# Loading K and V two heads at a time, with half as many keys per head in a loop step, in a decode attention kernel

## The chip, the cores and the metric

One core of a Trainium2 chip (the rounds of runs fell on several chips; a ratio compares kernels of the same round). The metric is the time of one execution on the device, in microseconds, taken over several executions. A profiled span is about 1.8 us shorter than the time (80.7 and 82.5 us for the kernel before). Runs marked slow (over 1.5% above the fastest of the same kernel) are left out of ratios.

## The reference

One token (D = 512) goes through layer norm; the result xn feeds an attention over the last 4096 keys of a cache and a small gated MLP. The output is the sum of both and the residuals.

```python
W = 4096                                  # window of the cache, Sk = 65536
q = (xn @ wq)                             # 32 heads of 128; wq is 4.2 MB in bf16
k = k_cache[:, :, Sk - W:, :]             # 8 heads of 4096 x 128: 8.4 MB
v = v_cache[:, :, Sk - W:, :]             # 8.4 MB; 4 query heads share one head of K and V
p = softmax(q @ k.T * 128 ** -0.5)
attn = (p @ v) @ wo                       # wo 4.2 MB
mlp  = (silu(xn @ w_gate) * (xn @ w_up)) @ w_down   # F = 1792, 1.8 MB each; scaled by sigmoid(xn . w_r)
out  = x + attn + xn + mlp
```

## The kernel before

30.7 MB come in through one queue in the order wq, K, V, gate, up, wo, w_down. Each head of K is one transfer of 1 MB: partition p holds 32 keys (8 KB) of that head.

```python
t_k = [dma(sy, f"k{g}", k_sb[:, g].rearrange("p b (i d) -> p (b i) d", d=DH),
           A_k_cache[0, g, Sk - W:, :].rearrange("(p t) d -> p t d", t=NT)) for g in range(HKV)]
```

The score loop takes one head per step. A head is four blocks of 1024 columns. Each block is copied into a buffer at a fixed address (C, VectorE), transposed on TensorE (T, eight transposes), copied out of PSUM (E, VectorE or ScalarE), and multiplied by q (Sm, two matmuls of 512 columns). In Sm the 32 weight columns are placed at one of four strips of the array, `tile_position=(0, 32 * cq)`:

```python
def Sm(b, i, q, last=False):
    te.wait_ge(s_ev[b], i)
    for e in range(2):
        c = 2 * b + e
        cq, ch = c % 4, c // 4                 # blocks 2 and 3: strips 0,1,2,3; so blocks 0 and 1
        ins = te.matmul(sc[32 * cq:32 * cq + 32, ch, :], lhsT=q[:], rhs=kT[:, b, e * 512:(e + 1) * 512],
                        start=False, stop=False, tile_position=(0, 32 * cq), skip_group_check=True)
    ...
with te.Fori(1, 9) as i:                       # one head per step
    T(0, i); T(1, i)
    te.wait_ge(s_qb, i); Sm(2, i, qB); Sm(3, i, qB, last=True)     # blocks of the step before
    T(2, i); T(3, i)
    te.wait_ge(s_qa, i); Sm(0, i, qA); Sm(1, i, qA, last=True)
```

Then softmax, a loop over heads for P times V (called PV; VectorE copies V and the probabilities into fixed buffers, TensorE multiplies, ScalarE brings the result back), gate and up, and 46 matmuls of one weight column (32 for wo, 14 for w_down).

## Time and profile before

| | before |
|---|---|
| time, median (lowest to highest), first 4 runs | 82.47 us (82.34 to 82.54) |
| profiled span | 80.7 us |
| first transpose of K | 16.52 us |
| scores ready | 42.49 us |
| PV done | 61.3 us |
| first wo matmul | 65.46 us |
| last piece of wo landed | 72.84 us |
| last matmul ended | 77.8 us |

In the timeline a line reads: start in us, length in us, engine, line of the kernel, operation, output<-inputs, how many instructions were merged, and in brackets how long the engine was idle before them and what ended that. The length of merged matmuls includes the latency of the last; the step to the next line's start tells the throughput.

### The profile page before, as it was taken

The numbers are of one execution on the slowest core, as the hardware profiler recorded it, in microseconds if no ns is written. First come the engines' busy times: TensorE is split into PE (matmuls) and PEld (weight loads), VectorE is DVE, ScalarE is ACT, GpSimd is POOL, SyncE is SP. The second block draws the span as 40 slices with busy tenths as digits, with TensorE's granted clock in tenths as the row PEclk, the third lists the DMA queues.
The fourth block names the chain that finished last, engine by engine and source line by source line (L and its number), as shares of the span: only waits on it lengthen the run. The fifth ranks groups of instructions, "written<-read, shape, count | busy, mean of one in ns | idle before, by whom it ended". The sixth has DMA issues, their size and how long they took to land.

```text
span 80.7 us, 1552 instructions
## 1 busy us (share of the span) xinstructions
PE 60.5 (75%) x596; PEld 29.9 (37%) x596; DVE 43.5 (54%) x103; ACT 29.7 (37%) x40; POOL 7.3 (9%) x27
## 2 busy tenths in 40 slices
PE   0012945589999999999988968877888887788950
PEld 0012201386657768667732323222233322123300
DVE  3775000195678977968736678888763380000030
ACT  1941001305696896895860422442222200000000
POOL 5910000101112112121200000000000000000000
PEclk9999999555799999999999999999999999999999
DMA  1899998999999999999999999999999999999400
GB/s 33 309 439 390 455 447 374 434 418 434 418 430 410 434 410 430 414 434 406 430 410 430 406 430 414 445 447 412 426 419 413 418 426 418 416 402 398 138 2 1
DMA packets 4185, 30.72 MB, mean 381 GB/s; under 512 B 467, under 2 KB 598, under 8 KB 1110
## 3 DMA queue, kind: packets, MB, share of 16 engines
q1 hardware_dynamic: 4178, 30.67, 91.7%
q8 instruction: 2, 0.03, 0.2%
q14 instruction: 1, 0.01, 0.0%
q10 hardware_dynamic: 4, 0.00, 0.0%
HBM read 30.67 MB, written 0.00 MB: 380 GB/s over the span
## 4 chain that ended last, share of the span: by engine, by line
SPq 48%; DMA 40%; PE 6%; issue 2%; DVE 1%
SPq L151 48%; DMA k_sb<-in_A_wo_dram 40%; PE ps L467 4%; PE ps L462 2%; DVE res L471 1%; SPq L500 0%; SPq L74 0%
## 5 line engine op out<-in xcount | busy, mean ns | idle before, releaser
L276 ACT COPY kT<-ps 128x1024 bf16<-128x1024 bf16 x19 | 18.5, 1019 | 8.8 <-PE ps L302 8.7
L302 PE MATMUL ps<-ident_bf,kin 128*128 128x128 bf16 x256 | 18.7, 231 | 0.8 <-DVE kin L268 0.6
L302 PEld LDWEIGHTS ps<-ident_bf,kin 128*128 128x128 bf16 x256 | 15.8, 104 | 5.1 <-issue 4.2
L268 DVE COPY kin<-k_sb 128x1024 bf16<-128x1024 bf16 x32 | 12.2, 422 | 0.7 <-PE ps L302 0.7
L273 DVE COPY kT<-ps 128x1024 bf16<-128x1024 bf16 x13 | 9.0, 692 | 4.4 <-PE ps L302 4.3
L462 PE MATMUL ps<-k_sb,oT 128*1 128x512 bf16 x32 | 7.5, 378 | 2.0 <-DMA k_sb<-in_A_wo_dram 2.0
L394 ACT CAST pvS<-ps 128x512 bf16<-128x512 f32 x8 | 4.7, 586 | 9.6 <-PE ps L399 9.6
L471 DVE TENSOR_TENSOR res<-ps,resid 1x512 bf16<-1x512 f32 x1 | 0.7, 679 | 11.5 <-PE ps L467 11.5
L375 DVE COPY vin<-v_sb 128x2048 bf16<-128x2048 bf16 x8 | 5.5, 686 | 1.4 <-PE ps L408 1.4
L381 DVE COPY vin<-v_sb 128x2048 bf16<-128x2048 bf16 x8 | 5.5, 683 | 0.0
L408 PE MATMUL ps<-vin,pTcur 128*16 128x512 bf16 x32 | 3.1, 381 | 2.6 <-ACT pvS L394 2.2
L462 PEld LDWEIGHTS ps<-k_sb,oT 128*1 128x1 bf16 x32 | 2.4, 83 | 7.1 <-DMA k_sb<-in_A_wo_dram 3.2
L420 PE MATMUL ps<-zmov,zst 128*128 128x512 bf16 x16 | 4.7, 377 | 0.0
L228 PE MATMUL ps<-wq_sb,xnT 128*1 128x512 bf16 x32 | 2.9, 499 | 2.3 <-DMA wq_sb<-in_A_wq_dram 2.3
L310 PE MATMUL ps<-kT,qB 128*32 128x512 bf16 x36 | 4.2, 413 | 0.4 <-ACT kT L276 0.3
L244 DVE COPY qpad<-ps 128x16 bf16<-128x16 bf16 x2 | 0.3, 174 | 7.6 <-PE ps L240 7.6
L310 PE MATMUL ps<-kT,qA 128*32 128x512 bf16 x32 | 4.4, 417 | 0.0
L259 POOL COPY qA<-qpad 128x32 bf16<-128x32 bf16 x8 | 2.0, 255 | 20.6 <-DVE qpad L244 10.9
L194 PE MATMUL ps<-ident_bf,xn_row 1*128 1x1 bf16 x4 | 0.3, 165 | 4.6 <-DVE xn_row L189 4.6
L147 PE MATMUL ps<-zmov,zst 128*128 128x512 bf16 x14 | 3.7, 382 | 0.0
L234 ACT CAST q<-ps 128x512 bf16<-128x512 f32 x2 | 1.1, 589 | 6.6 <-PE ps L228 6.6
L414 PE MATMUL ps<-vin,pTcur 128*16 128x512 bf16 x32 | 3.1, 382 | 0.2 <-DVE vin L381 0.2
(85 smaller groups left out, 50.2 us busy)
## 6 DMA issues: line engine op xcount, KB each, us to landing
k_sb<-in_A_k_cache_dram SPq DMA_DIRECT2D x8, 1024.0 KB, 20.6
v_sb<-in_A_v_cache_dram SPq DMA_DIRECT2D x8, 1024.0 KB, 28.2
wq_sb<-in_A_wq_dram SPq DMA_DIRECT2D x2, 2048.0 KB, 9.5
k_sb<-in_A_wo_dram SPq DMA_DIRECT2D x4, 1024.0 KB, 32.0
wq_sb<-in_B_w_gate_dram SPq DMA_DIRECT2D x1, 1792.0 KB, 29.3
wq_sb<-in_B_w_up_dram SPq DMA_DIRECT2D x1, 1792.0 KB, 31.4
k_sb<-in_B_w_down_dram SPq DMA_DIRECT2D x2, 512.0 KB, 31.4
k_sb<-in_B_w_down_dram SPq DMA_DIRECT2D x1, 384.0 KB, 25.7
```

Source lines behind the costliest of these rows:

```text
L147: te.matmul(ps[:, 7, :], lhsT=zst[:], rhs=zmov[:], start=True, stop=True)
L151: eng.dma_start(out=out_, in_=in_).then_inc(s, 16)
L268: ve.tensor_copy(out=kin[:, b, :], in_=k_sb[:, g, b, :]).then_inc(s_c[b], 1)
L273: ve.tensor_copy(out=kT[:, b, :], in_=tp[:, b, :]).then_inc(s_ev[b], 1)
L276: ac.copy(out=kT[:, b, :], in_=tp[:, b, :]).then_inc(s_ev[b], 1)
L302: ins = te.transpose(tp[:, b, k * P:(k + 1) * P], kin[:, b, k * P:(k + 1) * P], ident_bf[:])
L310: ins = te.matmul(sc[32 * cq:32 * cq + 32, ch, :], lhsT=q[:], rhs=kT[:, b, e * 512:(e + 1) * 512], start=False, stop=False, tile_position= ...
L375: ve.tensor_copy(out=vin[:, 0], in_=v_sb[:, g, 0:16, :]).then_inc(s_va, 1)
L381: ve.tensor_copy(out=vin[:, 1], in_=v_sb[:, g, 16:32, :]).then_inc(s_vb, 1)
L394: ac.copy(out=pvS[:].rearrange("p t d -> p (t d)"), in_=pv_ps).then_inc(s_pvs, 1)
L420: te.matmul(ps[:, 7, :], lhsT=zst[:], rhs=zmov[:], start=True, stop=True)
L462: te.matmul(a_ps, lhsT=oT2[:, j:j + 1], rhs=wo_sb[:, j * D:(j + 1) * D], start=False, stop=False, skip_group_check=True)
```

## The change

Its intent is longer pieces in the transfers: two heads of K (or V) in one transfer of 2 MB, in which partition 2q + h holds 64 keys of head h, 16 KB in a row. A step of the score loop then has 32 keys of each of 64 partitions of two heads, and the two heads need different queries. So each block's two matmuls now separate the even and odd partitions (e), with their own weights. Softmax works on two banks, one for each e. In the PV loop the probabilities are multiplied by a 0/1 column per parity.

```diff
-    t_k = [dma(sy, f"k{g}", k_sb[:, g]..., A_k_cache[0, g, Sk - W:, :].rearrange("(p t) d -> p t d", t=NT)) for g in range(HKV)]
+    def pair(cache, g):
+        return cache[0, 2 * g:2 * g + 2, Sk - W:, :].rearrange("h (q t) d -> q h (t d)", t=TP)   # TP = 64
+    t_k = [dma(sy, f"k{g}", halves(k_sb, g), pair(A_k_cache, g)) for g in range(HP)]             # HP = 4; V alike
 ...
-            c = 2 * b + e
-            cq, ch = c % 4, c // 4
-            ins = te.matmul(sc[32 * cq:32 * cq + 32, ch, :], lhsT=q[:], rhs=kT[:, b, e * 512:(e + 1) * 512],
-                            start=False, stop=False, tile_position=(0, 32 * cq), skip_group_check=True)
+            ins = te.matmul(sc[32 * b:32 * b + 32, e, :], lhsT=qAB[:, e, :],
+                            rhs=kT[:, b, :].rearrange("d (k h q) -> d h k q", h=2, q=PH)[:, e],
+                            start=False, stop=False, tile_position=(0, 32 * b), skip_group_check=True)
 ...
-    ac.activation(out=p_sb[:, h * 512:(h + 1) * 512], in_=sc[:, h, :], func=ACTF.Exp, ...)
+    ac.activation(out=p_sb[:].rearrange("p (j e) -> p e j", e=2)[:, h], in_=sc[:, h, :], func=ACTF.Exp, ...)
 ...
-        ve.tensor_copy(out=pTcur[:]..., in_=pT_ps...[:, :, :, REP * g:REP * (g + 1)]).then_inc(s_pt, 1)
+        for e in range(2):
+            ins = ve.tensor_scalar(out=pTcur[:, :, :, e, :], in0=src, scalar1=par2[:, e:e + 1], scalar2=None, op0=ALU.mult)
```

Cut are the setup of the 0/1 columns and of a permuted identity, the single q buffer, the maximum and bias of softmax for two banks, a sum over the two parities after the PV loop, and the shapes that follow from these.

## The prediction

> **What bounds the kernel now.** I read the strip of the span in 40 slices first, then the chain that ended last, then the timeline of the tail, and at last the timeline of TensorE in the score loop.
>
> ```profile
> PE   0012945589999999999988968877888887788950
> DVE  3775000195678977968736678888763380000030
> DMA  1899998999999999999999999999999999999400
> ...
> 40.85 31.95 DMA k_sb<-in_A_wo_dram
> 72.80 0.04 issue
> 72.84 1.89 PE ps L462 x8
> 74.73 3.10 PE ps L467 x14
> ```
>
> The DMA row is full from 4 us to 75 us, and the chain is one queue of 30.7 MB whose last piece of wo lands at 72.8; then 22 matmuls run one behind the other, and an add. So the transfers set the end. The span is 80.7 us, the time 82.48, so I add 1.8 us to a span. The rate by stage, from windows cut where the summed bytes of the slices change tensor (columns: window, length, engines, granted clock, DMA share, GB/s):
>
> ```profile
> 4.00:12.10 8.10, 3.68 (x24) 1.21 (x24) 2.75 (x10) 1.21 (x3) 0.35 (x2) 1.00 1.02 435
> 12.10:52.10 40.00, 35.22 (x411) 21.74 (x412) 27.75 (x65) 22.16 (x27) 3.90 (x16) 0.91 1.01 420
> 52.10:60.60 8.50, 6.93 (x74) 2.18 (x71) 6.79 (x15) 3.00 (x6) 0.00 (x0) 1.00 1.01 428
> 60.60:70.60 10.00, 8.06 (x64) 2.78 (x63) 3.19 (x7) 1.06 (x2) 0.00 (x0) 1.00 1.00 419
> ```
>
> These are wq (16 KB pieces) 435, K and V (8 KB) 420, gate and up (14 KB) 428, wo (8 KB) 419: longer pieces run some 3% faster. But compute is close behind. Of TensorE's timeline in the score loop (start, length, instructions merged):
>
> ```profile
> 28.00 0.40 PE L310 MATMUL ps<-kT,qB 128*32 128x512 bf16 x4
> 28.33 1.07 PE L302 MATMUL ps<-ident_bf,kin 128*128 128x128 bf16 x16
> 29.33 0.73 PE L310 MATMUL ps<-kT,qA 128*32 128x512 bf16 x4
> ...
> 65.46 1.89 PE L462 MATMUL ps<-k_sb,oT 128*1 128x512 bf16 x8 [0.26 <-DMA k_sb<-in_A_wo_dram]
> ```
>
> Half a loop step is 16 transposes (1.00 us to the next start) and four score matmuls (0.33 us to the next start): 1.33 us, or up to 1.8 where ScalarE's copy is late. Four matmuls of 512 columns take 0.33 us from start to next start, while eight of wo take 1.89 us (7 spacings of 0.216 plus a last of 0.38). Four in 0.33 us cannot have run one by one: they sat on four different 32-column strips (cq = 0, 1, 2, 3) and ran together.
>
> The slack follows: wo's first three pieces need 24 x 0.216 = 5.2 us of TensorE before 72.84, so its start may slip from 65.43 to 67.6 before anything is lost. **Slack 2.2 us.**
>
> **What the Trainium skill says.** "TensorE: Matmul & The Clock Gate", Part 3 (packing small matmuls): matmuls at different tile positions overlap, starting about 4 ns apart, and matmuls start and end strictly in program order. The trace agrees on the overlap (four in 0.33 us). "TensorEngine Tiling (Array Packing)", Key Properties: tiles operate independently; thus matmuls of one strip have nothing to overlap with, as the 0.216 us spacing of wo shows. The first page's Part 1 says that an idle TensorE is given half its clock and wins it back after some 3.4 us of work; here the clock was 0.50 from about 14.3 to 21.2 us, after the idle time that ended at 13.1. "DMA: Bandwidth & Descriptors", Latency and other measured facts, warns of rows at large powers of two; the two heads lie 16 MB apart. No run here shows that yet, and within a head the pieces stay contiguous.
>
> **The change part by part.**
>
> 1. Pieces of 16 KB for K and V: 16.8 MB at 420 GB/s is 39.9 us, at 432 (my choice between 428 and 435) 38.8. The queue shortens by **1.1 us**, if the rate is a matter of piece length.
>
> 2. A first pair must land whole. The shortest time from issue to landing on the K buffer is 13.7 us, and the first K was issued at 1.86: head 0 landed at 15.6, just before the first copy at 16.04. A second MB takes 2.5 us more: 18.0. The first transpose goes from 16.52 to 18.5: **+2.0 us** for compute. Later pairs land every 4.9 us and a pair takes over 7 us of compute, so no further wait.
>
> 3. The score matmuls. Before, block b's two matmuls went to strips 2b and 2b+1 (modulo 4). Now both go to strip b, one for each half of the partitions, in the order 2, 2, 3, 3 (and 0, 0, 1, 1). In program order the second must wait for the first; the third runs beside the second; the fourth waits for the third: three turns in place of one, two more of 0.216 us. A half step is 1.00 + 0.33 + 0.43 = 1.76 us. That also covers ScalarE: five copies of about 1 us in two steps of 3.5. At half clock it is 1.82 (16.52 to 18.34) + 0.55 + 2 x 0.43 = 3.23 us. I take one and a half half steps at half clock (it lasted 4.7 us from the first transpose before; the gate's phase is not known). Sixteen half steps: 1.5 x 3.23 + 14.5 x 1.76 = 30.4 us, where before they took 41.26 - 16.52 = 24.7. **+5.7 us**, with the tail of the scores unchanged.
>
> 4. Softmax: two bias columns and a strided output of the exponential, nothing I can size; all eight transposes wait for the second exponential, **+0.2**. The memset of the output bank (0.48 us) goes, but it was off the path.
>
> 5. The PV loop: a step takes 1.67 us, closed through VectorE's two value copies (0.69, 0.68), the probability copy (0.22), and TensorE and ScalarE. One copy of 128 columns becomes two multiplies by a 0/1 column; consecutive starts of such short operations lie 0.13 us apart, so **+0.14 x 8 = +1.1 us**. The matmuls have 32 columns of weights in place of 16 and the same stream, so 0.33 us still.
>
> 6. Setup: three more VectorE operations (about 0.28 + 0.28 + 0.15) and two more copies of q lie while wq and the first K pair are still on their way: nothing. A single q buffer is refilled during 1.00 us of transposes (copy 0.2 to 0.3 us): nothing.
>
> Sum: compute is later by 2.0 + 5.7 + 0.2 + 1.1 = 9.0 us at the end of PV, 61.26 + 9.0 = 70.3. From there to the first wo matmul it was 4.17 us, of which 0.5 and 0.26 were waits for up and wo, which have landed by now: 3.4, so 73.7. All of wo and nearly all of w_down are there (72.8 and 77.3 less 1.1). Then 46 matmuls: 45 x 0.216 + 0.38 = 10.1, to 83.8, against 77.8 before. **+6.0 us, of which I keep 5.7**, since small waits of the old loop may be absorbed: 82.48 + 5.7 = **88.2 us**. The 1.1 us saved on the queue is not seen, because the end no longer hangs on it.
>
> **The rivals.**
>
> - *The transfers stay the bound.* If compute slipped by under 2.2 us, the end would come 1.1 us earlier: 81.4 us. For it: the DMA row is full, and later wo pieces are each waited for 0.5 to 0.6 us. Against: the first pair alone costs 2.0, and the doubling on one strip is in the diff.
> - *Two matmuls of one strip cost one turn more, not two* (TensorE finding more overlap): 16 x 0.216 = 3.5 us less, 84.7. Against: the order 2, 2, 3, 3 and starts in order.
> - *No overlap at all (four turns)*: +3.5, about 91.7. Against: gate's 16 matmuls took 0.93 us, which needs overlap whenever the strips differ.
> - *Heads 16 MB apart slow the transfers.* At 10% less rate K and V take 4.4 us longer, and w_down lands at 82; then both ends meet near 88. For it only a warning of the skill.
>
> **Range and chances.** The clock's phase is worth 1.5 us either way, the PV step 1 us, the number of turns 3.5 us at small odds. I take 85.2 to 90.4 for 8 in 10, mostly between 86.5 and 89.5. Slower by over 2% (above 84.1) 0.90; within 2% 0.07, which is the rival with two turns and a lucky clock; faster 0.03, for which nearly every step would have to be wrong.
>
> **What would show each step right or wrong.** In the changed kernel's trace: K and V at about 432 GB/s; the first transpose near 18.5 us; four score matmuls spread over some 0.83 us in place of 0.40 and half steps of 1.76; scores ending near 50 us (42.5 before); PV ending near 70; no DMA wait before wo, the DMA row empty over the last 6 us or more, and 46 matmuls in one row of about 10 us. I am wrong if the score matmuls still merge into 0.40 us, if half steps stay at 1.33, or if a DMA is still what wo waits for last.

## More of the kernel before

The lines that carry the reading are in the prediction. Here only the PV loop of the kernel before, TensorE's timeline, of which the prediction has the numbers but not the lines; first matmuls of two successive steps lie 1.68 us apart:

```profile
49.58 0.39 PE L408 MATMUL ps<-vin,pTcur 128*16 128x512 bf16 x4 [0.31 <-ACT pvS L394]
...
51.26 0.39 PE L408 MATMUL ps<-vin,pTcur 128*16 128x512 bf16 x4 [0.31 <-ACT pvS L394]
```

## The result

The changed kernel takes 85.64 us (85.20 to 86.28, 4 runs) against 82.47: a ratio of 1.039, interval 1.031 to 1.047, slower. A ratio is the mean time of one kernel's fast runs over that of the other's fast runs of the same rounds, so it is not quite the ratio of these medians. Two later measurements of the same kernel gave 1.031 (85.75 us) and 1.031 (85.41 us). The prediction was 88.2 us, 85.2 to 90.4: the direction held and the time lies in the range, but at its low end. Of 5.7 us only some 3 came.

From the page of the changed kernel, the span and the slices, with the row of TensorE's granted clock (the share of its full clock that it was given, in tenths):

```profile
span 83.5 us, 1538 instructions
...
PE   0010956709999999999999893798887889999960
...
PEclk9999999999999999999999999759999999999999
DMA  2899999999999999999999999999999999980000
...
PE 59%; DMA 19%; DVE 9%; ACT 6%; issue 2%; SPq 1%; DVEq 0%
```

The DMA row now ends four slices (over 8 us) before the span does, and the last line, the engines' shares of the chain that ended last, puts 59% on TensorE; before, 88% of it was the queue (48% the issuing of its transfers, 40% a transfer of wo). The same window as for K and V before, now to 51.0 us (same columns):

```profile
12.10:51.00 38.90, 34.01 (x362) 20.13 (x362) 23.46 (x55) 21.64 (x25) 2.40 (x8) 1.00 1.01 429
```

429 GB/s in place of 420: the transfers did what was wanted of them. TensorE's timeline, from the score loop, the PV loop and the tail:

```profile
18.62 1.89 PE L316 MATMUL ps<-perm_bf,kin 128*128 128x128 bf16 x16 [1.92 <-DVE kin L282]
20.44 1.04 PE L322 MATMUL ps<-kT,qAB 128*32 128x512 bf16 x4
...
28.18 1.07 PE L316 MATMUL ps<-perm_bf,kin 128*128 128x128 bf16 x16
29.17 0.61 PE L322 MATMUL ps<-kT,qAB 128*32 128x512 bf16 x4
29.72 1.07 PE L316 MATMUL ps<-perm_bf,kin 128*128 128x128 bf16 x16
...
58.36 0.40 PE L419 MATMUL ps<-vin,pTcur 128*32 128x512 bf16 x4 [0.32 <-ACT pvS L406]
...
60.13 0.40 PE L419 MATMUL ps<-vin,pTcur 128*32 128x512 bf16 x4 [0.32 <-ACT pvS L406]
...
70.55 7.07 PE L476 MATMUL ps<-k_sb,oT 128*1 128x512 bf16 x32
77.46 3.19 PE L481 MATMUL ps<-k_sb,hTr 128*1 128x512 bf16 x14
```

The first transpose comes at 18.62. The four score matmuls take 0.61 us and 0.55 us to the next start (0.40 and 0.33 before); a half step is 1.54 us. A step of the PV loop is 1.77 us here, and 1.80 on average of the five from 56.58 to 65.57 (1.68 before). All 32 matmuls of wo run in one row from 70.55 with no wait for a transfer. The first half step and part of the second ran at half speed (16 transposes in 1.89 and 1.57 us, not 1.07), although the row of the granted clock reads full there. The kept trace has no record of the clock before 22.51 us, and the page shows full where there is none; so I go by the durations.

### The profile page after: what moved, and what is told of

Read it like the earlier page. It is cut to its first block, busy times and chain, and to the rows that moved or that the text cites. A ratio compares the mean times of both kernels' runs of the same rounds, so it can differ in the third digit from the quotient of the medians.

```text
span 83.5 us, 1538 instructions
## 1 busy us (share of the span) xinstructions
PE 64.1 (77%) x596; PEld 30.7 (37%) x596; DVE 46.3 (55%) x116; ACT 30.4 (36%) x40; POOL 6.0 (7%) x19
## 4 chain that ended last, share of the span: by engine, by line
PE 59%; DMA 19%; DVE 9%; ACT 6%; issue 2%; SPq 1%; DVEq 0%
PE ps L316 21%; DMA k_sb<-in_A_k_cache_dram 19%; PE ps L322 11%; PE ps L476 8%; PE ps L481 4%; PE ps L425 3%; ACT pvS L406 3%; PE ps L419 3%; DVE vin L392 2%; PE ps L431 2%; ACT p_sb L368 2%; PE ps L453 2%; PE ps L410 2%; DVE vin L384 2%; DVE pTcur L390 1%
## 5 line engine op out<-in xcount | busy, mean ns | idle before, releaser
L316 PE MATMUL ps<-perm_bf,kin 128*128 128x128 bf16 x256 | 18.4, 229 | 1.9 <-DVE kin L282 1.9
L316 PEld LDWEIGHTS ps<-perm_bf,kin 128*128 128x128 bf16 x256 | 15.6, 103 | 9.0 <-issue 6.8
L322 PE MATMUL ps<-kT,qAB 128*32 128x512 bf16 x68 | 11.5, 398 | 0.2 <-ACT kT L290 0.2
L431 PE MATMUL ps<-zmov,zst 128*128 128x512 bf16 x16 | 5.6, 435 | 0.0
L419 PE MATMUL ps<-vin,pTcur 128*32 128x512 bf16 x32 | 3.4, 415 | 2.2 <-ACT pvS L406 1.3
L275 POOL COPY qAB<-qpad 128x64 bf16<-128x64 bf16 x8 | 2.4, 300 | 37.2 <-PE ps L322 37.2
L243 PE MATMUL ps<-wq_sb,xnT 128*1 128x512 bf16 x32 | 3.8, 621 | 1.7 <-DMA wq_sb<-in_A_wq_dram 1.7
L390 DVE TENSOR_SCALAR pTcur<-ps,par 128x128 bf16<-128x128 bf16 x16 | 3.8, 279 | 1.6 <-PE ps L373 1.6
L425 PE MATMUL ps<-vin,pTcur 128*32 128x512 bf16 x32 | 3.5, 430 | 0.4 <-DVE vin L392 0.3
L151 PE MATMUL ps<-zmov,zst 128*128 128x512 bf16 x14 | 3.7, 382 | 0.0
```

Source lines behind the costliest of these rows:

```text
L316: ins = te.transpose(tp[:, b, k * P:(k + 1) * P], kin[:, b, k * P:(k + 1) * P], perm_bf[:])
L322: ins = te.matmul(sc[32 * b:32 * b + 32, e, :], lhsT=qAB[:, e, :], rhs=kT[:, b, :].rearrange("d (k h q) -> d h k q", h=2, q=PH)[:, e], sta ...
L419: ins = te.matmul(pv_ps[32 * tl:32 * tl + 32, :], lhsT=pTcur[:, tl].rearrange("p q e r -> p (q e r)"), rhs=vin[:, 0].rearrange("p (q t) d ...
L425: ins = te.matmul(pv_ps[32 * tl:32 * tl + 32, :], lhsT=pTcur[:, 4 + tl].rearrange("p q e r -> p (q e r)"), rhs=vin[:, 1].rearrange("p (q t ...
L431: te.matmul(ps[:, 7, :], lhsT=zst[:], rhs=zmov[:], start=True, stop=True)
```

## The experiments

Every kernel gave a correct result. "First wo matmul" is the best single mark of how late compute is, since all that follows it is a fixed row unless a transfer is late.

**The changed kernel again (e1, later e10).** No edit; the measure for the others.

> The changed kernel again, as the measure for the others on this chip. 85.6 us (85.2 to 86.3 so far), ratio to before 1.039. TensorE has four score matmuls in two turns (0.54 us to the next start), not three.

> The changed kernel once more for its scatter: 84.5 to 86.3 us, ratio 1.03 to 1.04. Its end hangs on compute, so where the half clock falls shows in the time; before hangs on the queue and stays within 0.5%.

85.75 us (84.56 to 85.91), ratio 1.031, and 85.41 us (84.51 to 86.23), ratio 1.031. The scatter is 1.6 to 2%, while the kernel before stays within 0.5% in all its runs. First wo matmul at 71.02 in the profile of e1. The profile of e10 fell in a slow run; nothing is drawn from it.

**Eight matmuls in one group (e4).** What do two matmuls of one strip cost? A turn is the time that one matmul of 512 columns holds its strip, 0.216 us. My prediction said two more turns; the half step of 1.54 in place of 1.33 says one. This kernel puts all eight score matmuls of a step behind each other, after all their waits.

```diff
-        T(0, i); T(1, i); Sm(2, i); Sm(3, i, last=True); T(2, i); T(3, i); te.wait_ge(s_q, i); Sm(0, i); Sm(1, i)
+        for b in range(4): T(b, i)
+        te.wait_ge(s_q, i)
+        for b in range(4): te.wait_ge(s_ev[b], i)
+        for b in range(4): Sm(b)                    # strips 0,0,1,1,2,2,3,3
```

> A measuring kernel, slower on purpose: all eight score matmuls of a step in one group, strips 0,0,1,1,2,2,3,3, after all waits. Three theories on order. Each strip goes its own way (a matmul of a free strip passes one that waits): two turns, 0.22 + 0.39 = 0.61 us from first start to last end. Neighbours in the program pair up: four turns, 1.04 us. Strict program order, as my prediction assumed: five turns, 1.26 us.

TensorE's timeline of one step, then (cut into stretches, of the score matmuls alone: window, length, TensorE busy and how many were in flight, weight loads, clock, DMA share, GB/s):

```profile
31.20 0.62 PE L321 MATMUL ps<-kT,qAB 128*32 128x512 bf16 x8 [1.22 <-ACT kT L292]
31.76 1.96 PE L316 MATMUL ps<-perm_bf,kin 128*128 128x128 bf16 x32
```

```profile
31.20:31.30 0.10, 0.10 (x4) 0.10 (x8) 1.00 0.77 328
31.30:31.40 0.10, 0.10 (x4) 0.03 (x5) 1.00 0.38 164
31.40:31.45 0.05, 0.05 (x8) 0.00 (x0) 1.00 0.77 328
```

Eight in 0.62 us: four start at 31.20, four more just after 31.40, while the first four still drain, and the transposes follow at 31.76. That is two turns, as if each strip were served by itself. Strict program order (five turns, 1.26 us) and pairs of neighbours (four, 1.04 us) are excluded. The records do not name which of the eight started first, so that a free strip's matmul passes a waiting one is inferred here from the count. The changed kernel's own trace shows it. In the group at 26.00 us the program has two matmuls for one strip, then two for another, and the second pair waits for ScalarE's copy (same columns; windows between the starts):

```profile
25.98:26.08 0.10, 0.08 (x1) 0.08 (x2) 1.00 0.76 328
26.11:26.21 0.10, 0.10 (x2) 0.10 (x2) 1.00 1.15 492
26.24:26.31 0.07, 0.07 (x3) 0.00 (x0) 1.00 0.00 0
```

Both weight loads of the first pair are there at once, but one matmul runs. At 26.10 (these times are of the trace's single records) the weight load that waits for the copy starts, and with it a matmul; the next comes at 26.22, 0.226 us after the first, and the last at 26.32, 0.226 us after the one of 26.10. So the third in the program started before the second, whose strip was taken.

As a kernel e4 is slow, 90.19 us in its one run, because TensorE waits for all four copies in each step.

**Four strips again (e2).** Only the strip of the odd partitions is changed, so that the four matmuls of a group stand on four strips; the PV loop reads those strips in reverse.

```diff
-            ins = te.matmul(sc[32 * b:32 * b + 32, e, :], lhsT=qAB[:, e, :], ..., tile_position=(0, 32 * b))
+            s = 3 - b if e else b
+            ins = te.matmul(sc[32 * s:32 * s + 32, e, :], lhsT=qAB[:, e, :], ..., tile_position=(0, 32 * s))
 ...
-            ve.tensor_scalar(out=pTcur[:, :, :, e, :], in0=src, ...)
+            ve.tensor_scalar(out=pTcur[:, :, :, e, :], in0=src[:, :, ::-1, :] if e else src, ...)
```

> Only the strip of the second half of the partitions is changed (block b of half 1 goes to strip 3-b), so that the four score matmuls of a group stand on four strips again. If strips shared by two matmuls are the largest cost: a group goes from 0.54 to 0.33 us to the next start, half steps from 1.54 to 1.33 to 1.4, 16 of them save 3.3 us of compute, and the end comes about 3.1 us earlier, 82.2 to 82.8. Rival, the cost is the strided read of the keys (64 columns at a stride of 128), which stays: the group stays near 0.54 and the time at 85.6.

83.85 us (83.19 to 83.89), ratio 1.013: 1.9 us less than e1. TensorE's timeline:

```profile
28.24 1.07 PE L316 MATMUL ps<-perm_bf,kin 128*128 128x128 bf16 x16
29.24 0.40 PE L323 MATMUL ps<-kT,qAB 128*32 128x512 bf16 x4
29.57 1.07 PE L316 MATMUL ps<-perm_bf,kin 128*128 128x128 bf16 x16
30.57 0.40 PE L323 MATMUL ps<-kT,qAB 128*32 128x512 bf16 x4
30.90 1.07 PE L316 MATMUL ps<-perm_bf,kin 128*128 128x128 bf16 x16
31.90 0.74 PE L323 MATMUL ps<-kT,qAB 128*32 128x512 bf16 x4
```

The group is back at 0.40 and 0.33, so the strided read of the keys costs nothing that shows. The saving is 1.9 and not 3.1, in part because every fourth group waits for ScalarE again (0.74 us, next transposes 0.79 after its start), as in the kernel before. From the first transpose to the last step's own score matmuls the loop takes 24.8 us here and 26.9 in e1. Sharing strips thus costs 2.1 us of loop. The turns alone come to 3.6 us (13 of 0.21 and two of 0.43 at half clock); late copies give back some 1.0 of it, and 0.5 is the clock, which in e2's profile was half for one half step more (transposes 1.55 us at 23.41; 1.07 at 24.26 in e1).

**The first pair of K in two transfers (e3).** Each has 32 keys of every partition, what one step needs; the other pairs stay.

```diff
-    t_k = [dma(sy, f"k{g}", halves(k_sb, g), pair(A_k_cache, g)) for g in range(HP)]
+    t_k0 = [dma(sy, f"k0{u}", *unit(A_k_cache, k_sb, 0, u)) for u in range(2)]      # 1 MB each, 8 KB pieces
+    t_k = t_k0 + [t for t in (dma(..., pair(A_k_cache, g)) for g in range(1, HP)) for u in range(2)]
```

> Only the first pair of K is loaded as two transfers of half the keys (8 KB pieces), the rest as in the change. If the wait for a whole first pair costs the full delay: first transpose at 16.5 to 16.7 in place of 18.6, and the time falls by 2.0 us to 83.6. Rival, the loop catches up on late data anyway: no gain, 85.6.

84.54 us (83.63 to 84.72), ratio 1.021 (1.014 to 1.027): 1.2 us less than e1 by the medians, though the lowest run of e1 (84.56) lies inside this range. The first transpose is at 17.47, not at 16.6: VectorE starts the first K copy at 17.00, right behind its last q copy, so now q sets the start. Its matmuls ran at half clock in this profile (16 of them in 1.88 us; 1.03 in the profile of before). The first wo matmul is at 69.65, 1.4 us before e1's. The wait for a whole first pair is confirmed as a cost; but of its 2.1 us only 1.15 came back, since q, late by its half clock, is next in line.

**Two heads to a transfer in the kernel before (e5).** The grain of the change alone: 2 MB transfers in the old layout, 8 KB pieces.

```diff
-    t_k = [dma(sy, f"k{g}", k_sb[:, g]..., A_k_cache[0, g, ...]) for g in range(HKV)]
+    t_k = [dma(sy, f"k{g}", <k_sb[:, 2g:2g+2]>, cache[0, 2 * g:2 * g + 2, ...].rearrange("h (p t) d -> p h (t d)", t=NT)) for g in range(4)]
```

> The kernel before with one part of the change alone: two heads to a transfer, but in its own layout (128 partitions per head, 8 KB pieces). First transpose 2.0 us later (18.5 in place of 16.5), the rate still 420 GB/s, and the wo matmuls start at about 67.4 in place of 65.4, just inside the slack of 2.2 us: 82.4 to 82.9 us. Rival, slack over-counted: up to 84.5.

82.59 us, ratio 1.000 (0.998 to 1.003). The first transpose came at 18.69, the first wo matmul at 66.99, 1.5 us later than before, and the last piece of wo was still waited for:

```profile
66.99 5.37 PE L465 MATMUL ps<-k_sb,oT 128*1 128x512 bf16 x24
72.98 1.89 PE L465 MATMUL ps<-k_sb,oT 128*1 128x512 bf16 x8 [0.62 <-DMA k_sb<-in_A_wo_dram]
```

Compute may be late by 1.5 us and nothing is lost: the slack is real, and at least that large.

**Four strips and a split first pair (e6).** Both edits.

> Four strips and the first pair of K in two transfers together. If the two savings (1.9 and 1.3 us) add, TensorE starts wo at about 67.7 and the time is 82.3 to 82.9; the DMA of wo is then close to setting the end again. Rival, they overlap, and 83.5 or more stays.

82.14 us (81.76 to 82.47), ratio 0.996 (0.994 to 0.999): the fastest version of all, by a little, and inside the 2% that count as the same. TensorE starts wo at 66.48, earlier than the 67.7 expected, and the time lies just below the range: the two savings add, with less of the half clock in this profile (no stretch of it in the PV loop). Its last piece of wo is waited for again (below), so the queue sets the end.

**The same with 8 KB pieces throughout (e7).** Every K and V transfer is a unit of 1 MB like those of e3.

> As the run with four strips and the split first pair, but every K and V transfer is 1 MB in 8 KB pieces (undoes the piece size alone, in the layout of the change). If piece length sets the rate: K and V back from 429 to 420 GB/s and the queue ends some 0.8 us later; the time is the same or up to 0.5 us longer than its fellow, since compute sets most of the end. Rival, the rate is not a matter of piece length: 429 stays.

82.60 us, ratio 1.002 (0.999 to 1.004). TensorE's last wo matmuls, first e6, then e7:

```profile
72.12 1.89 PE L483 MATMUL ps<-k_sb,oT 128*1 128x512 bf16 x8 [0.30 <-DMA k_sb<-in_A_wo_dram]
```

```profile
72.95 1.89 PE L481 MATMUL ps<-k_sb,oT 128*1 128x512 bf16 x8 [0.61 <-DMA k_sb<-in_A_wo_dram]
```

With 16 KB pieces the last of wo is there 0.83 us earlier (K and V at 428 GB/s from 12.1 to 51.0, against 420 in e7), and the time is 0.46 us shorter. The transfers of e7 are also half as large, but size is not it: e5, with 2 MB transfers of 8 KB pieces, has 420 GB/s in the same window. The three windows, e6, e7 and e5 (columns as in the prediction):

```profile
12.10:51.00 38.90, 33.38 (x387) 20.92 (x388) 25.96 (x64) 21.80 (x26) 2.31 (x8) 1.00 1.01 428
12.10:51.00 38.90, 33.38 (x387) 21.00 (x388) 26.01 (x64) 21.77 (x26) 2.02 (x8) 1.00 1.01 420
12.10:51.00 38.90, 33.22 (x377) 21.08 (x378) 24.75 (x59) 21.08 (x25) 3.90 (x16) 1.00 1.01 420
```

So the length of the pieces is worth 0.83 us of queue, the gain that the change was made for.

**Idle matmuls (e8).** Four before the second half of wq and four after the transposes of q, into an unused bank.

```diff
+            fill(2)            # after the first half of wq
 ...
+    fill(2)                    # ahead of the score loop
```

> The changed kernel with idle matmuls added (four before the second half of wq, four after the transposes of q), which change no result. If TensorE runs at half clock there only because it idles: the second half of wq takes 1.0 us in place of 1.9, the first transposes run at 1.07 us for 16 in place of 1.9, scores end about 1.7 us earlier, and the time falls to about 84. Rival, the clock does not react: 85.7 as before.

85.01 us, in two groups: 83.74, 83.79 and 84.72, and three of 85.3 to 85.4 that count as slow. Ratio of the fast ones 1.021. In the profile, of a run of 83.74, the first transposes ran at full speed, but the clock fell later:

```profile
18.60 1.07 PE L318 MATMUL ps<-perm_bf,kin 128*128 128x128 bf16 x16 [1.56 <-DVE kin L283]
19.60 0.61 PE L324 MATMUL ps<-kT,qAB 128*32 128x512 bf16 x4
...
51.73 1.01 PE L433 MATMUL ps<-zmov,zst 128*128 128x512 bf16 x2
```

Scores end at 44.8 (47.4 in e1), and at 51.7 two matmuls of 512 columns take 1.01 us in place of 0.59. The second half of wq took 1.47 us, not the 1.0 expected: the first record of the clock, full, is at 14.2 us, in the middle of it. In this profile the first transposes ran at full clock with the idle matmuls and at half clock without them; one profile is all there is, and why the clock falls in the PV loop in some runs stays open. The slow runs were not profiled.

**All three (e9).** Four strips, split first pair, idle matmuls in wq only.

> Four strips, the first pair of K in two transfers, and four idle matmuls between the two halves of wq. With them the wq and first transposes run at the full clock, the first transpose comes at 16.6, and wo could start at 65.5 or earlier; the queue with its 16 KB pieces then sets the end (last wo piece lands at about 72.1): 81.7 to 82.1 us and less scatter than without the idle matmuls. Rival: since the queue already set the end at 82.1 in the version without them, no gain, or the idle matmuls only move the slow clock to a later stage.

82.49 us (81.97 to 83.28), ratio of the fast runs 0.996 (0.993 to 1.000): no gain on e6, and a scatter of 1.6%, not less as expected. In the profiled run (82.87):

```profile
21.85 0.74 PE L330 MATMUL ps<-kT,qAB 128*32 128x512 bf16 x4
24.93 1.89 PE L323 MATMUL ps<-perm_bf,kin 128*128 128x128 bf16 x16 [2.35 <-DVE kin L289]
```

The loop started at 16.87 at full clock, used up the first pair by 22, and then stood still for the second, which VectorE could copy only at 24.45. After that gap the transposes ran at half clock (1.89 us). Earlier compute ran into the grain of the transfers. In e6 the second pair was copied at 23.05; why it landed 1.4 us later here I cannot say.

## Why the prediction was right or wrong

The direction and the reason were right: compute took over from the queue, at the places named. The size was off in one term above all. By the steps of the prediction, from the profile of the changed kernel:

| step | predicted | measured |
|---|---|---|
| 1. rate of K and V | 432 GB/s, queue 1.1 us shorter | 429; 0.83 us shorter (e7 against e6) |
| 2. first transpose | 18.5, +2.0 us | 18.62, +2.1 |
| 3. sixteen half steps | 30.4 us, +5.7 | 26.7 us (18.62 to 45.32), +2.0 |
| 4. softmax | +0.2 us | 46.56 to 51.91, 5.35 us against 4.87: +0.5 |
| 5. PV loop | +1.1 us | 51.91 to 67.22, 15.3 us against 13.9: +1.4 |
| PV to first wo matmul | 3.4 us | 3.3 us |
| first wo matmul | 73.7 | 70.55, +5.1 |
| 46 matmuls | 10.1 us | 10.1 us |

5.1 us less the slack of 2.2 is 2.9; the last matmul ended 2.84 us later, and the span grew by 2.8.

**The failed step is 3**, "three turns in place of one": the runs showed two (e4). A warm half step took 1.56 us on average (14 in 21.9 us from 23.46), not 1.76, which is 2.8 us of the 3.7 missed. Most of the other 0.9 is the same turn at half clock: the first half step, all of it at half speed, took 2.79 us (18.62 to 21.41), not 3.23. With two turns in place of three the prediction's own sum gives 1.5 x 2.80 + 14.5 x 1.54 = 26.6 us; measured 26.7. Its guess of one and a half half steps at half clock was thus close, by luck as much as by reading, since e1 had two. I took the rule of strict program order from the Trainium skill ("TensorE: Matmul & The Clock Gate", Part 3) and laid it over a case in which two matmuls of one strip follow each other, where no trace of the kernel before had shown it. The rival with one turn more, at 84.7 us, had the right mechanism, and I gave it small odds. That 85.6 still lay inside my range was the width of the range; the middle of it rested on the wrong count.

Step 2 was right in size; that splitting the pair wins back only 1.15 us of it, e3 shows. Step 4 missed that the exponentials take 0.84 and 0.81 us (0.69 and 0.68 before); their output is strided now, but no run varies that alone. In step 5 the clock was 0.50 from 53.2 to 56.6 us; in e1, with none of that, PV took 15.0 us (52.71 to 67.69), +1.05, as predicted. No run undoes the PV multiplies alone, so their cost is read from the traces. Of the slack of 2.2 us, e5 confirms 1.5. Two small slips changed nothing: step 5 read 0.13 us and multiplied 0.14, and the half clock of the kernel before ran from 14.47 to 21.29 us by the trace's records, the last 4.8 us of it under work without a gap, not the "some 3.4" quoted.

Rival "the transfers stay the bound": wrong here, but with strips and first pair mended it is what e6 and e7 show. Rival "heads 16 MB apart slow the transfers" (the caution in "DMA: Bandwidth & Descriptors", Latency and other measured facts): no sign of it, the rate rose.

What stays open is the phase of the clock. Since the end of the changed kernel hangs on TensorE, each run's half-clock stretches show in its time, which fits its scatter of 2%; the kernel before has such stretches too, hidden behind the queue. Only single runs were profiled, so this is argued, not shown. The mean clock doesn't settle it: among the 14 runs of the changed kernel 1.00 stands beside 84.51 us and beside 86.28. But that mean misses stretches: it is 1.00 for e1's profiled run too, whose first two half steps took 2.8 us each.

## What to carry to other kernels

A change that speeds the bound by 2% is worth 2% only while everything behind it keeps up: count the slack of the second path first (here 2.2 us by my count, of which 1.5 is shown), then what the change adds to it. When a layout changes, look at which matmuls stand side by side on the array: the same four matmuls took 0.33 or 0.55 us depending on one index. Double the size of a transfer and its first consumer waits for the double; splitting only the first one, together with the strips, brought the change level with the kernel before (ratio 0.996).

## What the Trainium skill lacked or had wrong

- "TensorE: Matmul & The Clock Gate", Part 3, calls matmuls strict first in, first out, in start and end. Eight matmuls in program order on strips 0,0,1,1,2,2,3,3 took 0.62 us, four starting at once and four about 0.22 us later; with starts in program order it would have been 1.26 by my count of turns. In the changed kernel's group at 26.00 us the third matmul of the program started at 26.10 and the second at 26.22. The page says nothing of two matmuls for one strip.
- "DMA: Bandwidth & Descriptors", Specifications, gives 512 B as the least transfer for line rate. In transfers of 1 to 2 MB, 8 KB pieces moved at 420 GB/s and 16 KB pieces at 428 to 429; no page has this 2%.
- "TensorE: Matmul & The Clock Gate", Part 1, warns in general that the clock's events in a trace are unreliable. It lacks the case seen here: the early records can be missing. In the changed kernel's trace the first is at 22.51 us and in e6's there is none, and the views then read 1.00 while 16 transposes took 1.89 us in place of 1.07. Durations are the better witness.
